# A second mixture whose conversions pass through a PSUM bank, and a table that paces them

## The chip, the cores and the metric

The kernel runs on one core of one Trainium2 chip. Its metric is the device time of one execution in microseconds. Three executions of the kernel before took 868.26, 870.14 and 873.36 us, with a median of 870.14.

## What is computed

Three blocks follow one another. Attention (4 batches, 8 heads, 576 positions, 64 wide) adds a strided and a local softmax; its output is a matrix x of 2304 tokens by 512. The first mixture has d_ff 768, the second 1536:

```python
def _moe_ref(x, w1, w2, w3, w_out) -> np.ndarray:
    h = np.maximum(np.maximum(x @ w1, x @ w2), x @ w3)
    return (h @ w_out).astype(np.float32)

def _moe2_ref(x, w_a, w_b, w_out) -> np.ndarray:
    a = x @ w_a
    b = x @ w_b
    return (a * b @ w_out).astype(np.float32)
```

Weights arrive as doubles (two 32-bit words each), and so have to be converted on the chip. Every float32 factor of a product is split in a rounded high part and a rest, so that three matmuls (high by high, rest by high, high by rest) stand for one.

## The kernel before

**Stages.** Attention runs to about 196 us with some first units of the first mixture under it. Then the order of instructions is written out by hand (`manual_schedule`, L1391). The first mixture works in quads (L1395): two chunks of 128 columns of d_ff by two blocks of 384 tokens, four units of three products `m1_p` (12 matmuls each), and the output of a quad by seven half-size products in two halves (`quad_out`, `product` L832), issued between the `m1_p` of the quad that follows. Before them `quad_forms` makes differences of the four hidden tiles y on VectorE (L762) and splits them on ScalarE and GpSimd (`part2`, L744, L745). Six quads are followed by four single units, the `rest` (L1396). In each `m1_unit` (L1446) a product is issued, then `tick(ticks[...])`, then outputs (`between`).

**Lanes.** What is not bound to a product stands in two lanes of generators (L636): conversions of weights, forms of weights (`quad_w`), forms of the second mixture's input (`sform`). `tick(n)` (L638) takes n steps from them, from one `yield` to the next, and so fixes where these instructions stand in the queues of VectorE, ScalarE and GpSimd. `need` (L657) takes steps until a missing piece is there. The numbers were FIRST (5 after each product of the first quad), MID and REST (L1436), and in the second mixture 1 or 2 after each product (`step`, `o`, L1519 to L1531).

**A conversion** (`convert_steps`, L509) of 128 by 512 doubles has four VectorE steps: two masks (L519 the exponent, L522 the mantissa into the tile `cm`), a multiply-add of the low word onto `cm` (L527) beside a ScalarE step on the exponent (L526), the sign (L529), and the product of mantissa and exponent (L536), into `cm` or into a tile `F` of forms. In the first mixture a cast on ScalarE (L630) and a rest on GpSimd (L632) are two further steps.

**The second mixture** (from about 445 us) runs 18 units of six blocks of d_ff by three pairs of token blocks. A unit (`m2_unit`, L1253) has seven products for each of the two weights j, in the order 1, 2, 6, 5, 7, 4, 3, six matmuls each (`prod`, L1052). Products 1, 6, 7 and 4 accumulate in a bank A (tag `ua`, two banks), 2 in a bank of its own, 5 and 3 in a bank E (both of tag `ub`, three banks in turn). `snap` (L1071) copies A to SBUF on ScalarE before the next product goes on in it. `m2_done` (L1078) adds bank and copy on VectorE: for j = 0 into `ca` (L1085), for j = 1 into `g` (L1095), and then multiplies `g` by `ca` (L1096). The hidden result is split (`m2_parts`, L1249, L1250) and multiplied by w_out one unit later (`m2_o`, tag `o`, three banks, added by VectorE at L1319). In all PSUM has eight banks: 2 `ua`, 3 `ub`, 3 `o`.

Every engine takes its instructions in the order of its queue. So a ScalarE copy that frees a bank for the next product can stand behind a step of a conversion that waits for VectorE.

## Time and profile before

| | before |
|---|---|
| median of three runs | 870.14 us |
| the profiled execution | 871.95 us |
| its span in the trace | 870.2 us |
| TensorE busy | 827.2 us, 95% |
| VectorE busy | 695.1 us, 80% |
| ScalarE busy | 357.7 us, 41% |
| GpSimd busy | 449.4 us, 52% |
| mean granted TensorE clock | 0.973 |

The span is the time from the first to the last instruction; 1.75 us lie around it. Busy times of matmuls overlap, since the trace models the end of each, so an idle TensorE in the trace was idle for a little longer in fact. An entry in square brackets is idle time of that engine just before the instruction, with the instruction that ended it.

### The profile page before, as it was taken

How to read it: one execution, taken by the hardware profiler on the slowest of the kernel's cores; microseconds unless marked ns; L12 is line 12 of the kernel's file. 1: busy time of each engine (PE TensorE's matmuls, PEld its weight loads, DVE VectorE, ACT ScalarE, POOL GpSimd, SP SyncE). 2: the span in 40 equal slices, each digit the busy share in tenths (PEclk: the TensorE clock that was granted, in tenths of full speed). 3: DMA queues.
4: the chain of work that ended last, by engine and by line, in shares of the span. 5: the costliest groups of instructions: out<-in, count | busy, mean ns of one | idle time of the engine just before them, and what ended most of it. 6: DMA issues, size and time to landing. Idle time of an engine off the chain costs nothing.

```text
span 870.2 us, 15404 instructions
## 1 busy us (share of the span) xinstructions
PE 827.2 (95%) x5785; PEld 772.2 (89%) x5785; DVE 695.1 (80%) x1220; ACT 357.7 (41%) x812; POOL 449.4 (52%) x417
## 2 busy tenths in 40 slices
PE   4898999999998999998998999999999999999998
PEld 3667788899898999997998899999999989999997
DVE  4799987666979588689589898999999865578885
ACT  3586655443333223324144554344434342343331
POOL 3776775544446237436357554545463563455541
PEclk9599899999999999999999999999999999999999
DMA  8977865310411113220134455445454449766612
GB/s 179 180 163 150 150 123 109 63 33 25 122 49 48 49 57 104 71 73 25 64 143 145 169 182 180 160 150 191 145 200 139 158 152 356 266 218 218 218 49 73
DMA packets 125557, 116.34 MB, mean 134 GB/s; under 512 B 81835, under 2 KB 108203, under 8 KB 125483
## 3 DMA queue, kind: packets, MB, share of 16 engines
q1 hardware_dynamic: 121162, 98.06, 38.7%
q10 hardware_dynamic: 4320, 17.30, 5.7%
q8 instruction: 45, 0.74, 0.4%
q14 instruction: 30, 0.24, 0.1%
HBM read 80.74 MB, written 34.60 MB: 133 GB/s over the span
## 4 chain that ended last, share of the span: by engine, by line
PE 69%; DVE 17%; DMA 4%; POOL 3%; issue 3%; ACT 2%; SPq 1%; DVEq 0%; POOLq 0%; ACTq 0%
PE ps_m L670 28%; PE ps_u L1061 25%; PE ps_m L1210 4%; PE ps_q L835 4%; DMA vr<-in_v_dram 3%; DVE cm L527 2%; DVE ce L529 2%; DVE cm L522 2%; DVE ce L519 1%; DVE cm L536 1%; PE ps_av L460 1%; PE ps_s L340 1%; PE ps_tl L423 1%; PE ps_sd L322 1%; PE ps_ud L438 1%
## 5 line engine op out<-in xcount | busy, mean ns | idle before, releaser
L670 PE MATMUL ps_m<-xh,w 128*128 128x384 f32 x864 | 175.0, 341 | 2.1 <-ACT t L696 1.6
L670 PEld LDWEIGHTS ps_m<-xh,w 128*128 128x128 f32 x864 | 152.4, 190 | 5.0 <-ACT t L696 2.7
L1061 PE MATMUL ps_u<-xh,w 128*128 128x384 f32 x720 | 137.5, 337 | 0.0
L1061 PEld LDWEIGHTS ps_u<-xh,w 128*128 128x128 f32 x720 | 125.8, 188 | 2.0 <-ACT sn L1073 0.6
L1061 PE MATMUL ps_u<-xl,w 128*128 128x384 f32 x648 | 123.9, 338 | 3.5 <-ACT sn L1073 3.5
L1061 PEld LDWEIGHTS ps_u<-xl,w 128*128 128x128 f32 x648 | 113.9, 189 | 5.6 <-ACT sn L1073 4.1
L1250 POOL TENSOR_TENSOR gl<-g,gh 128x384 fp32r<-128x384 f32 x52 | 58.6, 1127 | 82.0 <-ACT gh L1249 68.8
L670 PE MATMUL ps_m<-xl,w 128*128 128x384 f32 x432 | 94.6, 337 | 1.8 <-POOL xl L484 1.8
L670 PE MATMUL ps_m<-wo,gh 128*128 128x512 f32 (+1 forms) x316 | 93.1, 392 | 0.4 <-DVE acc L1319 0.4
L1073 ACT COPY sn<-ps_u 128x384 f32<-128x384 f32 x108 | 50.5, 478 | 97.6 <-PE ps_u L1061 97.4
L670 PEld LDWEIGHTS ps_m<-xl,w 128*128 128x128 f32 x432 | 76.3, 188 | 2.2 <-POOL xl L484 2.0
L670 PEld LDWEIGHTS ps_m<-wo,gh 128*128 128x128 f32 x316 | 58.6, 188 | 10.3 <-DVE acc L1319 0.8
L527 DVE SCALAR_TENSOR_TENSOR cm<-raw,cm 128x512 f32<-128x512 uint32 x60 | 64.1, 1069 | 1.5
L526 ACT ACTIVATE ce<-ce,ebias 128x512 int16<-128x512 uint16 x60 | 43.4, 723 | 46.8 <-DVE ce L519 46.6
L699 DVE TENSOR_TENSOR t<-ps_m,t 128x384 f32<-128x384 f32 x48 | 26.4, 551 | 44.5 <-PE ps_m L670 42.1
L992 POOL TENSOR_TENSOR w<-F,w 128x768 fp32r<-128x768 f32 (+1 forms) x36 | 56.8, 1592 | 4.9 <-ACT w L990 4.4
L1319 DVE TENSOR_TENSOR acc<-ps_m,acc 128x512 f32<-128x512 f32 (+1 forms) x67 | 44.8, 675 | 14.1 <-PE ps_m L670 14.0
L1003 POOL TENSOR_TENSOR F<-F 128x256 f32<-128x256 f32 x24 | 19.5, 815 | 65.3 <-DVE F L536 54.3
L670 PE MATMUL ps_m<-wo,gl 128*128 128x512 f32 (+1 forms) x158 | 48.9, 391 | 0.0
L1249 ACT CAST gh<-g 128x384 fp32r<-128x384 f32 x52 | 26.7, 514 | 52.9 <-DVE g L1096 49.2
L529 DVE SCALAR_TENSOR_TENSOR ce<-raw,ce 128x512 uint16<-128x512 uint16 x60 | 45.6, 760 | 2.5 <-ACT ce L526 2.5
L519 DVE TENSOR_SCALAR ce<-raw 128x512 uint16<-128x512 uint16 x60 | 45.2, 753 | 2.8 <-DMA raw<-in_moe_w_dram 2.8
(204 smaller groups left out, 1711.6 us busy)
## 6 DMA issues: line engine op xcount, KB each, us to landing
dw<-w SPq DMA_DIRECT2D x24, 768.0 KB
raw<-in_moe_w_dram SPq DMA_DIRECT2D x18, 512.0 KB
raw<-in_moe_w_out_dram SPq DMA_DIRECT2D x18, 512.0 KB
w<-dw SPq DMA_DIRECT2D x12, 768.0 KB
w<-dw ACTq DMA_DIRECT2D x12, 768.0 KB
dw<-wo SPq DMA_DIRECT2D x12, 512.0 KB
vw<-in_v_dram SPq DMA_DIRECT2D x62, 80.0 KB
vr<-in_v_dram SPq DMA_DIRECT2D x16, 288.0 KB
```

The lines of the kernel that those rows point to most:

```text
L519: nc.vector.tensor_scalar(out=e, in0=top, scalar1=0x7FF0, scalar2=None, op0=ALU.bitwise_and)
L526: nc.scalar.activation(out=s16, in_=e, func=AF.Relu, bias=ebias, scale=8.0)
L527: nc.vector.scalar_tensor_tensor(out=f, in0=lo, scalar=2.0**-32, in1=m, op0=ALU.mult, op1=ALU.add)
L529: nc.vector.scalar_tensor_tensor(out=e, in0=top, scalar=0x8000, in1=e, op0=ALU.bitwise_and, op1=ALU.bitwise_or)
L670: nc.tensor.matmul(ps, lhs[a], rhs[b], start=(i == 0), stop=(i == n - 1))
L835: nc.tensor.matmul(ps, sw[c0, n][a][:, m * P : (m + 1) * P], hq[n][b], start=start and k == 0, stop=k == 2, skip_group_check=not start,)
L992: nc.gpsimd.tensor_tensor(out=l, in0=w, in1=h.bitcast(F32), op=ALU.subtract)
L1061: nc.tensor.matmul(ps, w[:, a, slot, kk], y[:, b * HK + kk], start=start and i == 0, stop=i == 3 * HK - 1, skip_group_check=not start,)
L1073: nc.scalar.copy(t, ps)
L1210: nc.tensor.matmul(y, lhs[a], tw[c, n][b], start=start and k == 0 and t == ts.start, stop=k == 2, skip_group_check=True,)
L1250: nc.gpsimd.tensor_tensor(out=l, in0=g, in1=h.bitcast(F32), op=ALU.subtract)
L1319: nc.vector.tensor_tensor(out=a, in0=ps, in1=a, op=ALU.add)
```

## The change

There are three parts. First, once the first mixture has closed its banks, a pool of one PSUM bank (`cs`) is opened. The mantissa of a conversion is masked into that bank, the multiply-add goes on in it in place, and the last step writes from it to its target: the form tile `F`, or for w_out's pieces `cm` in SBUF. The exponent stays in SBUF. The bank comes from `ub`, which has two in place of three. Second, in `m2_done` for j = 1 the sum of bank and copy is written back into the bank, and the multiply reads it there; this holds for two of the three sums of a unit, not for (1, 1), whose bank goes on to accumulate. Third, the fixed numbers of `tick` are replaced by a table PACE of 330 entries, taken one after each product or output; when it has ended, the old numbers hold. 84 entries are the first mixture's, 21 each those of the first units of the second mixture, and those of units 3 to 6 are, in their effect, the old numbers.

```diff
@@ -46,6 +46,19 @@
 SUM_ACT = (0, 1, 2, 3, 4, 6, 7, 8, 9, 10, 13, 14, 15)
 NORM_POOL = (0, 1, 2, 3, 4, 5, 6, 7, 8, 9, 10, 11, 13, 14, 15)
 ADD_PSUM = range(16)
+
+
+PACE = (
+    14, 0, 4, 2, 5, 1, 3, 4, 2, 7, 1, 1, 2, 1, 0, 5, 5, 6, 1, 3, 5, 6, 4, 1, 0, 0, 1, 0, 4, 0, 4, 4, 1, 0, 3, 0,
+    0, 2, 0, 3, 8, 1, 1, 5, 0, 3, 4, 2, 0, 0, 0, 3, 7, 2, 5, 6, 3, 1, 0, 0, 0, 0, 3, 2, 4, 4, 2, 4, 7, 5, 1, 0, 1,
+    1, 0, 4, 1, 1, 8, 1, 4, 1, 5, 2, 1, 1, 0, 0, 3, 2, 4, 0, 0, 3, 0, 4, 0, 0, 2, 4, 0, 1, 0, 0, 0, 0, 5, 0, 4, 0,
+    0, 0, 2, 3, 6, 0, 1, 2, 0, 0, 3, 2, 1, 2, 0, 0, 0, 0, 1, 3, 0, 0, 7, 2, 0, 2, 2, 1, 3, 0, 1, 1, 1, 0, 1, 1, 0,
+    1, 1, 1, 1, 1, 1, 2, 2, 2, 2, 1, 1, 2, 2, 1, 1, 2, 2, 0, 0, 0, 1, 1, 1, 1, 1, 1, 2, 2, 2, 2, 1, 1, 2, 2, 1, 1,
+    2, 0, 1, 1, 0, 1, 1, 1, 1, 1, 1, 2, 2, 2, 2, 1, 1, 2, 2, 1, 1, 2, 2, 0, 0, 0, 1, 1, 1, 1, 1, 1, 2, 2, 2, 2, 1,
+    1, 2, 2, 1, 1, 2, 0, 1, 1, 0, 0, 4, 0, 4, 1, 0, 2, 1, 0, 4, 2, 0, 4, 1, 0, 0, 0, 1, 4, 2, 0, 0, 1, 3, 0, 1, 1,
+    4, 0, 0, 3, 3, 0, 0, 6, 0, 0, 2, 0, 0, 4, 0, 0, 1, 0, 2, 0, 2, 3, 0, 5, 1, 2, 1, 3, 1, 0, 0, 2, 1, 0, 1, 0, 2,
+    0, 0, 3, 3, 0, 0, 1, 0, 2, 1, 2, 3, 4, 0, 1, 1, 2, 2, 1, 0, 0, 1, 1, 1, 1, 0, 0, 0, 0, 0, 0, 0, 0, 0, 1,
+)
 
 
 @with_exitstack
@@ -514,7 +527,14 @@
         late_n[0] += "p" in late
         pl = late["p"] if late_n[0] % 2 else rawp
         e = pl.tile([P, NP_], U16, tag="ce", name="ce", bufs=CB)
-        m = pl.tile([P, NP_], U32, tag="cm", name="cm", bufs=CB)
+        fin = w
+        if w is None or "c" not in psp_:
+            m = pl.tile([P, NP_], F32, tag="cm", name="cm", bufs=CB)
+            if w is None:
+                fin = m
+        if "c" in psp_:
+            m = psp_["c"].tile([P, NP_], F32, tag="cs", name="ps_c", bufs=1)
+        m = m.bitcast(U32)
         s16, f = e.bitcast(I16), m.bitcast(F32)
         nc.vector.tensor_scalar(
             out=e, in0=top, scalar1=0x7FF0, scalar2=None, op0=ALU.bitwise_and
@@ -530,11 +550,11 @@
             out=e, in0=top, scalar=0x8000, in1=e, op0=ALU.bitwise_and, op1=ALU.bitwise_or
         )
         yield
-        out, i0, i1 = f if w is None else w, f, e.bitcast(BF16)
+        i0, i1 = f, e.bitcast(BF16)
         if w is not None and len(w.shape) == 3:
             i0, i1 = (x.rearrange("p (a b) -> p a b", a=w.shape[1]) for x in (i0, i1))
-        nc.vector.scalar_tensor_tensor(out=out, in0=i0, scalar=2.0**-20, in1=i1, op0=ALU.mult, op1=ALU.mult)
-        yield f
+        nc.vector.scalar_tensor_tensor(out=fin, in0=i0, scalar=2.0**-20, in1=i1, op0=ALU.mult, op1=ALU.mult)
+        yield fin
 
     def split(h, l, w):
 
@@ -653,6 +673,11 @@
             else:
                 return did
         return did
+
+    pace = iter(PACE)
+
+    def beat(n=0):
+        tick(next(pace, n))
 
     def need(has, key):
 
@@ -1091,9 +1116,10 @@
             g = gw[c % 2][:, x * TB : (x + 1) * TB]
         else:
             g = late["p"].tile([P, TB], F32, tag="g", name="g", bufs=2)
+        s = g if (i, b) == (1, 1) else ps
         if t is not None:
-            nc.vector.tensor_tensor(out=g, in0=ps, in1=t, op=ALU.add)
-        nc.vector.tensor_tensor(out=g, in0=ps if t is None else g, in1=ca.pop((i, b)), op=ALU.mult)
+            nc.vector.tensor_tensor(out=s, in0=ps, in1=t, op=ALU.add)
+        nc.vector.tensor_tensor(out=g, in0=s, in1=ca.pop((i, b)), op=ALU.mult)
         if strassen_o(c, p) and (i, b) == (0, 1):
             lanes[0].append(g_forms(c))
         else:
@@ -1264,7 +1290,7 @@
             T1[j] = snap(A[j])
             yield
         for j in range(2):
-            b = bank_u("ub", 3)
+            b = bank_u("ub", 2)
             prod(b, c, p, j, 2, True)
             m2_done(c, p, j, 0, 0, b, T1[j])
             yield
@@ -1273,7 +1299,7 @@
             T2[j] = snap(A[j])
             yield
         for j in range(2):
-            E[j] = bank_u("ub", 3)
+            E[j] = bank_u("ub", 2)
             prod(E[j], c, p, j, 5, True)
             yield
         for j in range(2):
@@ -1433,7 +1459,6 @@
         (5, 5): ("x", 5),
     }
     OUTS = (0, 4, 3, 3, 2, 2)
-    FIRST, MID, REST = (5,) * 12, (1, 1, 2, 2, 3, 3, 5, 5, 5, 5, 5, 5), (0, 0, 1, 3, 3, 3, 5, 5, 4, 2, 2, 2)
     outs, forms = None, None
 
     def between(n):
@@ -1443,14 +1468,14 @@
             next(outs)
         next(forms, None)
 
-    def m1_unit(u, steps, n, ticks):
+    def m1_unit(u, steps, n):
         for f in at_unit.get(u, ()):
             f()
         for j in range(3):
             next(steps)
             if j == 2 and n == 0 and outs is None and pending:
                 m1_o(*pending.pop())
-            tick(ticks[3 * n + j])
+            beat()
             between(3 * n + j)
         if u in after_unit:
             opened.add(after_unit[u])
@@ -1459,22 +1484,23 @@
         hq, y = {}, {}
         steps = quad(c0, c1, b0, b1, hq, y)
         for n, u in enumerate(((c0, b0), (c0, b1), (c1, b0), (c1, b1))):
-            m1_unit(u, steps, n, FIRST if c0 == 0 else MID)
+            m1_unit(u, steps, n)
         if outs is not None:
             assert next(outs, None) is None
         outs, forms = quad_out(c0, c1, b0, b1, hq), quad_forms(hq, y)
         next(forms)
     for n, u in enumerate(rest):
         steps = dense(u)
-        m1_unit(u, steps, n, REST)
+        m1_unit(u, steps, n)
         next(steps, None)
     for x in outs, forms:
         assert next(x, None) is None
     opened.add(("w", 2))
     m1_ps.close()
+    psp_["c"] = ctx.enter_context(tc.tile_pool(name="psc", bufs=1, space=PSUM, reuse_waits="tile"))
     psp_[2] = ctx.enter_context(tc.tile_pool(name="psm2", bufs=1, space=PSUM, reuse_waits="tile"))
 
-    psp_[2].tile([P, 512], F32, tag="ub", name="ps_u", bufs=3)
+    psp_[2].tile([P, 512], F32, tag="ub", name="ps_u", bufs=2)
 
     def spill(blk):
         y2[blk] = dram.tile([P, NK * TB], F32, tag=f"y2{blk}", name=f"y2{blk}")
@@ -1519,7 +1545,7 @@
         def step(m, k_=1):
             for _ in range(m):
                 part(lambda: next(unit, None))
-                tick(k_)
+                beat(k_)
 
         def one_o():
             while prev_o and next(prev_o[0], StopIteration) is StopIteration:
@@ -1528,7 +1554,7 @@
         def o(m):
             for _ in range(m):
                 part(one_o)
-                tick(2)
+                beat(2)
 
         step(3)
         if n == 0:
@@ -1567,7 +1593,7 @@
             for m in (0, 1, 1, 1, 2, 1, 1, 1):
                 step(m)
                 part(one_o)
-                tick()
+                beat(1)
             load_in(c + 2, 0)
             while prev_o:
                 part(one_o)
```

## Rows read from the trace of the kernel before

**Rows 1.** The page, part 1: busy us, share of the span, instructions.

```profile
PE 827.2 (95%) x5785; PEld 772.2 (89%) x5785; DVE 695.1 (80%) x1220; ACT 357.7 (41%) x812; POOL 449.4 (52%) x417
```

**Rows 2.** Windows by stage: width; busy us of each engine; granted clock; DMA share; GB/s.

```profile
196.00:285.00 89.00, 83.77 (x511) 80.52 (x510) 73.31 (x114) 34.19 (x71) 44.26 (x38) 1.00 0.20 60
...
390.00:500.00 110.00, 98.52 (x519) 94.79 (x518) 90.45 (x122) 42.58 (x77) 63.09 (x45) 0.95 0.30 108
500.00:690.00 190.00, 190.00 (x993) 176.83 (x993) 175.65 (x264) 81.97 (x154) 96.88 (x82) 1.00 0.48 172
690.00:710.00 20.00, 19.38 (x102) 17.62 (x101) 15.71 (x21) 9.14 (x17) 13.06 (x8) 1.00 0.21 68
```

**Rows 3.** Timeline of PE: start, us, line, out<-in, count, [idle before <-releaser].

```profile
236.57 0.62 PE L835 MATMUL ps_m<-hh,wo 128*128 128x384 f32 x2 [1.91 <-DVE y L699]
...
272.64 1.66 PE L670 MATMUL ps_m<-xh,w 128*128 128x384 f32 x8 [1.46 <-ACT t L696]
...
276.13 0.59 PE L835 MATMUL ps_q<-gh,w 128*128 128x384 f32 x2 [1.13 <-DVE acc L830]
...
410.09 0.58 PE L835 MATMUL ps_q<-gh,w 128*128 128x384 f32 x2 [3.40 <-DVE acc L830]
...
436.13 0.61 PE L670 MATMUL ps_m<-hh,wo 128*128 128x384 f32 x2 [2.76 <-DVE t L699]
...
460.95 3.50 PE L1061 MATMUL ps_u<-xl,w 128*128 128x384 f32 x12 [3.20 <-ACT sn L1073]
...
484.92 3.56 PE L1061 MATMUL ps_u<-ys,w 128*128 128x384 f32 x12 [1.99 <-ACT sn L1073]
```

**Rows 4.** Timeline of DVE: first step of a conversion, and the maximum after it.

```profile
232.26 0.42 DVE L519 TENSOR_SCALAR ce<-raw 128x512 uint16<-128x512 uint16 x1
...
235.96 0.55 DVE L699 TENSOR_TENSOR y<-ps_m,t 128x384 f32<-128x384 f32 x1
```

**Rows 5.** Timeline of ACT at 271 us.

```profile
271.18 0.62 ACT L630 CAST w<-cm 128x512 fp32r<-128x512 f32 x1 [3.66 <-DVE cm L536]
```

**Rows 6.** Timeline of DVE at 402 us.

```profile
402.15 0.55 DVE L699 TENSOR_TENSOR t<-ps_m,t 128x384 f32<-128x384 f32 x1
```

**Rows 7.** Timeline of DVE, 431 to 436 us.

```profile
431.07 2.08 DVE L522 TENSOR_SCALAR cm<-raw 128x512 uint32<-128x512 uint32 x1
...
435.52 0.55 DVE L699 TENSOR_TENSOR t<-ps_m,t 128x384 f32<-128x384 f32 x1
```

**Rows 8.** Timeline of ACT ahead of the snaps, 459 to 484 us.

```profile
459.81 0.72 ACT L526 ACTIVATE ce<-ce,ebias 128x512 int16<-128x512 uint16 x1 [5.13 <-DVE ce L519]
...
483.78 0.72 ACT L526 ACTIVATE ce<-ce,ebias 128x512 int16<-128x512 uint16 x1 [2.71 <-DVE ce L519]
```

**Rows 9.** Timeline of DVE, 456 to 479 us.

```profile
456.39 2.32 DVE L529 SCALAR_TENSOR_TENSOR ce<-raw,ce 128x512 uint16<-128x512 uint16 x1
...
473.38 1.62 DVE L1096 TENSOR_TENSOR g<-g,ca 128x384 f32<-128x384 f32 x1
...
476.46 2.22 DVE L536 SCALAR_TENSOR_TENSOR cm<-cm,ce 128x512 f32<-128x512 f32 x1
```

**Rows 10.** Groups by line and shape, DVE: count | busy us, mean ns | idle before.

```profile
L527 DVE SCALAR_TENSOR_TENSOR cm<-raw,cm 128x512 f32<-128x512 uint32 x60 | 64.1, 1069 | 1.5
...
L522 DVE TENSOR_SCALAR cm<-raw 128x512 uint32<-128x512 uint32 x60 | 44.9, 748 | 0.0
...
L1096 DVE TENSOR_TENSOR g<-g,ca 128x384 f32<-128x384 f32 x39 | 32.8, 841 | 1.3
...
L536 DVE SCALAR_TENSOR_TENSOR cm<-cm,ce 128x512 f32<-128x512 f32 x36 | 29.4, 817 | 0.6
...
L1096 DVE TENSOR_TENSOR g<-ps_u,ca 128x384 f32<-128x384 f32 x13 | 7.1, 547 | 1.5 <-PE ps_u L1061 0.7 <-POOL gl L1250 0.5 <-ACT ca L1083 0.3
```

**Rows 11.** Timeline at 703 us: a unit's products 2 (PE), the sum of the unit before (DVE).

```profile
703.04 2.24 PE L1061 MATMUL ps_u<-xh,w 128*128 128x384 f32 x12
...
703.21 0.54 DVE L1085 TENSOR_TENSOR ca<-ps_u,sn 128x384 f32<-128x384 f32 x1
```

## The prediction, made before the change was run

> **What bounds the kernel now.** The page first: TensorE is busy for 827.2 of 870.2 us, VectorE for 695.1 [rows 1]. So no edit of VectorE's work can be worth more than the time in which TensorE waits. The windows by stage say where that is [rows 2]. From 500 to 690 us TensorE is busy for 190.00 of 190 us: whatever VectorE saves there is worth nothing. Idle are 89.00 - 83.77 = 5.2 us at the start of the first mixture, 11.5 us from 390 to 500 and 0.6 us around 700. From 390 to 500 the granted clock is also 0.95 of full, against 1.00 around it; 0.05 of 110 us is 5.5 us at half its higher level, 1.2 in place of 2.4 GHz. Before 196 us nothing is edited. The timeline of TensorE then names the gaps [rows 3]: A 1.91 (at 236.6 us), B 1.46 and 1.13 (272 to 276), C 3.40 (410), D 2.76 (436), E 3.20 (461), F 1.99 (485). With G, the 0.62 near 700, that is 16.5 us of waiting, and with the slow clock 22 us: the ceiling of this change, unless it shortens TensorE's own work, which it doesn't touch. After C, E and F the clock is low; behind E and F twelve matmuls take 3.50 and 3.56 us [rows 3] where 2.24 is usual [rows 11], 1.3 us each in these alone. 5.5 us over three falls is at most 1.8 each; I take 1.6.
>
> Each gap is a queue: TensorE needs a bank, and the instruction that frees it stands on VectorE or ScalarE behind steps of a conversion or a form.
>
> **The table, gap by gap.** I count steps: a conversion of the first mixture has six, and one takes 235.96 - 232.26 = 3.7 us of VectorE [rows 4].
>
> A: the maximum that frees the bank ended at 236.5, right behind the sixth conversion of the first quad [rows 4]. The old numbers take all 49 steps that the first quad is offered. The table's first twelve entries (14, 0, 4, 2, 5, 1, 3, 4, 2, 7, 1, 1) sum to 44, one of which finds nothing to take, and leave six: just this conversion, which goes to 2, 1, 0, 5 behind the next quad's first products. The maximum comes 3.7 us earlier, more than the gap. Gain 1.9. What is late next is VectorE in the second quad, where 89.00 - 73.31 = 15.7 us are free in that stage [rows 2].
>
> B: the copy that frees the bank stands on ScalarE behind a weight cast, which waited 3.66 us for the last step of a conversion [rows 5]. The table (6, 4, 1 in place of 5, 5, 5 in the last unit of this quad) hands out only the second step of that conversion there, so the 1.46 should go. But VectorE has about the same work ahead of the differences, TensorE arrives 1.9 us earlier because of A, and then the sum that ends the 1.13 is awaited for longer. Of 2.6 I take 0.5; bounds 0 and 2.6.
>
> C: VectorE comes to a maximum of the last quad only at 402.15 [rows 6], because the input's forms and a conversion stand before it, and the differences and the sum that ends the gap come after it. The table gives two steps of a conversion, 1.07 for L527 [rows 10] and some 0.7 for L529, to the products before, but concentrates a form's three large steps and a conversion's last in one beat (2, 4, 7 in place of 5, 5, 5). All is still issued ahead of that maximum. I take 0.7 of 3.40; from -1.5 (bunching) to 3.4 plus its clock.
>
> D: one beat of five steps put a whole conversion (its second mask alone 2.08 us [rows 7]) ahead of the maximum at 435.52, with VectorE idle before it. The table gives 8, 1, 4: two steps of it come a product earlier, one stands there, the last follows. Two masks and the multiply-add, 2 x 0.75 + 1.07 = 2.6 us by their means [rows 10] and more by the 2.08 of this one, are out of the way: 2.8, the whole of D.
>
> **PSUM for mantissa and sums.** E and F are of another kind: TensorE waits for a snap on ScalarE, and the snap waits behind the exponent's step, which itself waited 5.13 and 2.71 us for VectorE's first mask [rows 8]. VectorE was late there because its instructions with both inputs in SBUF were drawn out beside a busy GpSimd: L529 took 2.32 us, L1096 1.62 and L536 2.22 [rows 9], the last two against means of 0.84 and 0.82 [rows 10]. The cost of an operand in PSUM can be read directly: the same multiply takes 841 ns with both factors in SBUF and 547 with one in PSUM [rows 10]. Of 36 multiplies (two in each of 18 units) each saves 0.294: 10.6 us. For a conversion's 512 columns I scale 547 by 512/384: 0.73, say 0.7. By the count of the table 30 of the 36 pieces of the second mixture are converted after the bank is opened; L522, L527 and L536 go from 748, 1069 and 817 ns [rows 10] to 0.7 each, 0.53 less, 16 us. Together 27 us off VectorE, nearly all beside a full TensorE. It counts only in the 11 us between 473 and 484: L1096 from 1.62 to 0.55 and L536 from 2.22 to 0.7 are 2.6 us, more than F's 1.99. For E there is the table too: in the first unit it spaces the next conversion over the pauses around products 5. I take F 2.0 + 1.6, and E 3.2 + 1.6 less 0.5 left over.
>
> No row shows VectorE writing to PSUM. Its price lies between the 547 of the read (0.73 scaled) and, if reading and writing one bank in place goes at half pace, twice that, 1.1 for a sum and 1.5 for a step of a conversion. I take the lower end, as L1096 is the nearest row; the upper end is a rival below.
>
> SBUF — State Buffer of the Trainium skill, section "Who interferes with whom", states that a VectorE instruction with at most one SBUF input and outside the two-port modes doesn't contend with GpSimd, and that otherwise the port pair is locked for a whole instruction. The 841 against 547 agrees. By that rule the exponent's mask L519 and its sign L529, which keep both sides in SBUF, go on waiting. VectorE: DVE Perf Modes, "Why PSUM operands drop a tier", speaks against the change: a mask into PSUM loses its double pace; by the 0.42 of the other mask in [rows 4] that would be 0.3 more for L522, 9 us less saved where VectorE isn't the limit.
>
> **The lost bank.** With two `ub` banks, product 2 of a unit takes the bank that product 3 of the unit before used, one product earlier than with three. The worst place I found is at 703: the product starts at 703.04, the sum that frees its bank ends at 703.75 [rows 11], a wait of 0.7. If three units had it, it would cost 2.1. With 27 us less on VectorE these sums come earlier. I set 1.0 for all new waits, those of bunched steps included, bounds 0 and 3. For G, where VectorE is late with w_out's sums, 0.4.
>
> **Sum.** 1.9 + 0.5 + 0.7 + 2.8 + 4.3 + 3.6 + 0.4 - 1.0 = 13.2 us. The profiled execution took 871.95 (span 870.2 and 1.75 around it), 0.2% above the median of 870.14. 871.95 - 13.2 = 858.7; on the median 856.9, so 857.
>
> **Rivals.**
> *All gaps go* (chance 0.12). B and C are freed too, and no bank is missed: 870.1 - 22 = 848. For it: VectorE has slack in every stage. Against: C's work is not reduced.
> *The wait moves* (0.17). GpSimd's instructions are as long as before, and what no longer waits in L527 or L536 waits in L519 and L529 next to them; L529 took 2.32 us [rows 9]. Then E and F stay, 7.5 of the 7.9 counted for them: 864.5. The Trainium skill's rule of the lock, named above, speaks for this.
> *The gaps only move* (0.07). Before 285 us and from 380 to 410 VectorE is the engine that is late, and handing out the same work elsewhere gives A back in B and lengthens C; with E or F staying, 868.
> *Slower: in place at half pace* (0.06). In the 190 us from 500 to 690 VectorE has 190.00 - 175.65 = 14.3 us free [rows 2]. At twice the price 24 conversions there cost (1.5 - 0.75) + (1.5 - 1.07) - 0.1 = 1.1 more each, 26 us, the 17 sums in place 0.55 each, 9 us, less 5 us of multiplies: 30. From 14.3 on VectorE is the limit, and the stage grows by some 16 us, with waits for `ub` in every unit. Less A and D: 870.1 + 16 - 4.7 = 881.
> The rest of the chance, 0.58, is the forecast's, with 851 to 863 as its own range.
>
> **How the numbers follow.** Under 0.5%, 4.4 us, this kernel can't be told from no change. Faster by more: the forecast, the first two rivals, less a share for values near the bound: 0.84. Within 0.5%: 0.10. Slower: 0.06. For 8 in 10 the range reaches over the forecast, half of the first rival and most of the second: 848 to 866.
>
> **What would show it.** A and D: no gap of TensorE over 0.5 us before 285 us but B's second, none between 425 and 440. E and F: no gap over 1 us from 450 to 490, a granted clock of at least 0.98 from 390 to 500. PSUM: L527 and L536 at 0.7 us with no spread, L1096 at 0.55 for all but the (1, 1) tiles, VectorE's sum below 675. Lost bank: no wait of `ps_u` for VectorE beyond 1 us in all. I would be wrong if C grew, if L519 and L529 took up what the others save, or if in-place sums took over 0.8.

## The result: 25 us shorter, nearly twice the forecast

| | before | after |
|---|---|---|
| median of four runs each | 871.75 us | 846.74 us |
| lowest and highest | 868.26 to 874.18 | 846.02 to 847.74 |
| span in the trace | 870.2 us | 845.9 us |
| mean granted TensorE clock | 0.973 | 0.980 |

The ratio is 0.9717, with a 95% interval of 0.9678 to 0.9756. The forecast was 857.0 with a range of 848 to 866: the direction held, the time lies 1.3 us below the range, and the sum, 13.2 us, found about half of the gain. It came out close to the rival in which all gaps go (848).

Lines of the kernel after: L519, L522, L526, L527, L529 and L536 of a conversion are L539, L542, L546, L547, L549 and L556; the maximum L699 is L724, its copy L696 L721, the differences L762 L787, the output sums L830 L855, the snap L1073 L1098, sum and multiply L1095 and L1096 L1121 and L1122, the matmuls L670, L835 and L1061 L695, L860 and L1086. In the experiments that carry a second table they lie 3 higher still.

The page of after, part 1 (busy us, share of the span, instructions) and the engines' shares of the chain of work that ended last:

```profile
PE 818.5 (97%) x5785; PEld 767.7 (91%) x5785; DVE 656.6 (78%) x1220; ACT 355.2 (42%) x812; POOL 444.0 (52%) x417
...
PE 85%; DMA 5%; POOL 4%; DVE 2%; SPq 2%; issue 1%; ACT 1%; POOLq 0%; DVEq 0%; ACTq 0%
```

VectorE has lost 38.5 us of its 695.1 [rows 1], and its share of the chain is 2%. Not all of this is PSUM's: by the pages of the two halves below, VectorE is busy for 672.3 us with PSUM alone and for 680.7 with the table alone, where the same instructions are only spaced otherwise. The same windows as before:

```profile
196.00:285.00 89.00, 88.63 (x546) 87.09 (x545) 72.03 (x119) 33.67 (x71) 44.76 (x38) 1.00 0.19 60
...
390.00:500.00 110.00, 108.73 (x597) 104.38 (x596) 87.09 (x142) 50.55 (x96) 69.50 (x53) 1.00 0.39 139
500.00:690.00 190.00, 190.00 (x998) 177.30 (x997) 155.66 (x258) 79.13 (x151) 97.58 (x80) 1.00 0.46 164
690.00:710.00 20.00, 20.00 (x102) 18.14 (x101) 9.32 (x15) 4.09 (x9) 4.38 (x5) 1.00 0.94 346
```

TensorE, the first busy time of each row, went from 83.77 to 88.63 of 89 us and from 98.52 to 108.73 of 110 us [rows 2], and the granted clock of the second stretch from 0.95 to 1.00. VectorE's 20 us less between 500 and 690 bought nothing: TensorE was full there already, and the starts compared below shift by 0.00 us there. What TensorE still waits for from 190 to 850 us, by the table of its waits (us in total, times, longest):

```profile
PE ps_m L695 <- DVE t L724: 0.7, 1, 0.7
PE ps_u L1086 <- ACT sn L1098: 0.4, 1, 0.4
PE ps_m L695 <- ACT xh L496: 0.3, 1, 0.3
```

1.4 us are left of some 17. No line has `ps_u` waiting for VectorE, so the lost `ub` bank shows no cost.

**What each gap gave.** Both kernels issue the same 5785 matmuls in the same order, so the start of the n-th in after can be set against the n-th in before; a step in this difference between two neighbours of a gap is what the gap gave. Starting from 196 us (attention is unchanged, and its end scatters by some us between executions). These are one trace of each kernel:

| place in before | forecast | measured | of it |
|---|---|---|---|
| A, 237 to 271 us | 1.9 | 3.6 | 2.1 at the gap, 1.5 in small waits behind it |
| B, 272 to 279 | 0.5 | 3.1 | 1.7 and 1.4 |
| C, 404 to 415 | 0.7 | 5.4 | 4.1 at the gap and just ahead of it, net of 0.2 lost at 377, and 1.3 slow clock behind it |
| D, 436 | 2.8 | 3.0 | |
| new waits, 437 to 450 | -1.0 | -1.3 | 0.9 for the maximum (the first line above, 0.7 of it idle), 0.3 and less |
| E, 461 to 466 | 4.3 | 4.4 | 2.9 and 1.5 slow clock |
| F, 485 to 490 | 3.6 | 3.8 | 2.2 and 1.6 slow clock |
| G and all behind it | 0.4 | 1.7 | 0.65, 0.55, 0.5 |

The rest of the 24.3 us between the spans, 0.6, is 1.1 in attention and behind the last matmul less a loss of 0.5 before 234 us, none of which the change explains.

**The price in PSUM.** VectorE's groups by line and shape in after (count | busy us, mean ns of one | idle before):

```profile
L549 DVE SCALAR_TENSOR_TENSOR ce<-raw,ce 128x512 uint16<-128x512 uint16 x60 | 49.8, 830 | 4.0 <-ACT ce L546 3.9
...
L539 DVE TENSOR_SCALAR ce<-raw 128x512 uint16<-128x512 uint16 x60 | 40.6, 677 | 2.2 <-DMA raw<-in_moe_w_dram 2.2
...
L547 DVE SCALAR_TENSOR_TENSOR cm<-raw,cm 128x512 f32<-128x512 uint32 x30 | 30.4, 1014 | 0.4
...
L1122 DVE TENSOR_TENSOR g<-ps_u,ca 128x384 f32<-128x384 f32 x39 | 21.7, 556 | 5.9 <-POOL gl L1276 1.1 <-issue 1.1 <-PE ps_m L1236 0.7
...
L547 DVE SCALAR_TENSOR_TENSOR ps_c<-raw,ps_c 128x512 f32<-128x512 uint32 x30 | 20.8, 692 | 0.7
L542 DVE TENSOR_SCALAR ps_c<-raw 128x512 uint32<-128x512 uint32 x30 | 20.5, 684 | 0.0
L1121 DVE TENSOR_TENSOR ps_u<-ps_u,sn 128x384 f32<-128x384 f32 x36 | 20.2, 562 | 10.2 <-PE ps_u L1086 10.2
...
L556 DVE SCALAR_TENSOR_TENSOR F<-ps_c,ce 128x512 f32<-128x512 f32 x20 | 13.8, 688 | 0.7
...
L1121 DVE TENSOR_TENSOR g<-ps_u,sn 128x384 f32<-128x384 f32 x13 | 7.2, 552 | 4.5 <-ACT sn L1098 4.5
```

Half of the conversions, those begun before the bank is opened (the first mixture's 24 and six of the second's 36), still have their mantissa in `cm` in SBUF: L547 costs 1014 ns there and 692 through the bank. A sum in place costs 562 ns, against 552 for the same sum written to SBUF and 547 for the multiply that only reads a bank [rows 10]. So the lower of the two bounds was right, and the rival at half pace is out.

### The profile page after: what moved, and what is told of

It reads as the page before. It is cut to its first block, busy times and chain, and to the rows that moved or that the text cites. A ratio compares the mean times of both kernels' runs of the same rounds, so it can differ in the third digit from the quotient of the medians.

```text
span 845.9 us, 15426 instructions
## 1 busy us (share of the span) xinstructions
PE 818.5 (97%) x5785; PEld 767.7 (91%) x5785; DVE 656.6 (78%) x1220; ACT 355.2 (42%) x812; POOL 444.0 (52%) x417
## 4 chain that ended last, share of the span: by engine, by line
PE 85%; DMA 5%; POOL 4%; DVE 2%; SPq 2%; issue 1%; ACT 1%; POOLq 0%; DVEq 0%; ACTq 0%
PE ps_m L695 39%; PE ps_u L1086 30%; PE ps_q L860 5%; PE ps_m L1236 4%; DMA vr<-in_v_dram 4%; PE ps_av L473 1%; PE ps_ud L451 1%; POOL vr L414 1%; PE ps_tl L436 1%; POOL el L403 1%; PE ps_sd L335 1%; PE ps_s L353 1%; PE ps_m L860 1%; DMA raw<-in_moe_w_dram 1%; PE ps_td L425 1%
## 5 line engine op out<-in xcount | busy, mean ns | idle before, releaser
L695 PE MATMUL ps_m<-xh,w 128*128 128x384 f32 x864 | 175.0, 341 | 0.3 <-ACT xh L496 0.3
L695 PEld LDWEIGHTS ps_m<-xh,w 128*128 128x128 f32 x864 | 152.8, 190 | 2.1 <-ACT xh L496 0.6
L1086 PE MATMUL ps_u<-xh,w 128*128 128x384 f32 x720 | 136.8, 336 | 0.1
L1086 PEld LDWEIGHTS ps_u<-xh,w 128*128 128x128 f32 x720 | 125.3, 188 | 1.9 <-DVE acc L751 0.4
L1086 PE MATMUL ps_u<-xl,w 128*128 128x384 f32 x648 | 122.4, 335 | 0.4 <-ACT sn L1098 0.4
L1086 PEld LDWEIGHTS ps_u<-xl,w 128*128 128x128 f32 x648 | 112.9, 188 | 2.2 <-ACT sn L1098 0.7
L1098 ACT COPY sn<-ps_u 128x384 f32<-128x384 f32 x108 | 51.1, 479 | 123.7 <-PE ps_u L1086 120.2
L1276 POOL TENSOR_TENSOR gl<-g,gh 128x384 fp32r<-128x384 f32 x52 | 55.4, 1066 | 82.3 <-ACT gh L1275 75.2
L695 PE MATMUL ps_m<-xl,w 128*128 128x384 f32 x432 | 95.2, 339 | 1.7 <-POOL xl L497 1.7
L695 PE MATMUL ps_m<-wo,gh 128*128 128x512 f32 (+1 forms) x316 | 92.4, 390 | 0.0
L695 PEld LDWEIGHTS ps_m<-xl,w 128*128 128x128 f32 x432 | 76.9, 189 | 2.1 <-POOL xl L497 2.0
L695 PEld LDWEIGHTS ps_m<-wo,gh 128*128 128x128 f32 x316 | 58.4, 188 | 9.6
L724 DVE TENSOR_TENSOR t<-ps_m,t 128x384 f32<-128x384 f32 x48 | 26.5, 551 | 45.6 <-PE ps_m L695 40.3
L546 ACT ACTIVATE ce<-ce,ebias 128x512 int16<-128x512 uint16 x60 | 43.4, 724 | 43.0 <-DVE ce L539 42.9
L1345 DVE TENSOR_TENSOR acc<-ps_m,acc 128x512 f32<-128x512 f32 (+1 forms) x67 | 44.9, 676 | 18.1 <-PE ps_m L695 17.9
L549 DVE SCALAR_TENSOR_TENSOR ce<-raw,ce 128x512 uint16<-128x512 uint16 x60 | 49.8, 830 | 4.0 <-ACT ce L546 3.9
L1110 DVE TENSOR_TENSOR ca<-ps_u,sn 128x384 f32<-128x384 f32 x54 | 30.0, 555 | 29.4 <-PE ps_u L1086 18.1
L695 PE MATMUL ps_m<-wo,gl 128*128 128x512 f32 (+1 forms) x158 | 48.9, 391 | 0.0
L1228 DVE TENSOR_TENSOR acc<-ps_m,acc 128x512 f32<-128x512 f32 (+1 forms) x62 | 33.3, 552 | 15.5 <-PE ps_m L1236 13.2
L539 DVE TENSOR_SCALAR ce<-raw 128x512 uint16<-128x512 uint16 x60 | 40.6, 677 | 2.2 <-DMA raw<-in_moe_w_dram 2.2
```

The lines of the kernel that those rows point to most:

```text
L539: nc.vector.tensor_scalar(out=e, in0=top, scalar1=0x7FF0, scalar2=None, op0=ALU.bitwise_and)
L546: nc.scalar.activation(out=s16, in_=e, func=AF.Relu, bias=ebias, scale=8.0)
L549: nc.vector.scalar_tensor_tensor(out=e, in0=top, scalar=0x8000, in1=e, op0=ALU.bitwise_and, op1=ALU.bitwise_or)
L695: nc.tensor.matmul(ps, lhs[a], rhs[b], start=(i == 0), stop=(i == n - 1))
L1086: nc.tensor.matmul(ps, w[:, a, slot, kk], y[:, b * HK + kk], start=start and i == 0, stop=i == 3 * HK - 1, skip_group_check=not start,)
L1098: nc.scalar.copy(t, ps)
```

## The experiments

Each edits the kernel after; OLD stands for the numbers of before written out as a table. The theory: the gaps A to D close by the table alone, E and F by what it and PSUM do together, and a gap costs more than the idle time printed beside it. The rivals: PSUM's relief of VectorE is the gain and the table only rides on it; or the table does all and PSUM is idle ornament. In these traces attention ends between 4.3 us earlier and 2.6 us later than in the trace of after, for no reason in the edits. So where medians lie close or their intervals overlap, what a part gives is read from the starts of matmuls behind attention. Only lines of each edit that matter are shown, `...` marks what is left out.

**The table alone, PSUM alone.** For the first, the sums and the mantissa go back to SBUF and the third `ub` bank returns; for the second, OLD replaces the table:

```diff
# e1_table_alone
-        s = g if (i, b) == (1, 1) else ps
+        s = g if t is not None else ps
...
-            b = bank_u("ub", 2)
+            b = bank_u("ub", 3)
...
-    psp_["c"] = ctx.enter_context(tc.tile_pool(name="psc", bufs=1, space=PSUM, reuse_waits="tile"))
...
# e2_psum_alone
...
+PACE = OLD
```

> Edit: of the change the table alone; mantissa and sums stay in SBUF, ub has three banks. Theory, that the table closes gaps A to D and PSUM closes E, F and G: the 16.5 us of waiting in the trace of before fall by A 1.9, B 2.6, C 3.4 and D 2.8, and C's fall of the clock (1.7) goes with it, so some 859 us; E and F stay with 3.2 and 2.0 and their low clock. Rival 1, that the table does nearly all: 847 to 849, no wait of TensorE over 1 us after 200 us. Rival 2, that the table only moves the waits without PSUM's relief: 866 or more.

> Edit: the changed kernel with the old numbers FIRST, MID, REST and 1 or 2 in place of the table; mantissa and sums in PSUM, ub two banks. Theory: everything before 445 us is as before, A to D stand with their 10.7 us, and E (3.2), F (2.0), G (0.6) and two falls of the clock go: some 862 us. Rival 1, that PSUM gives nothing that counts: 869 to 873, E and F as before. Rival 2, that the lost bank shows when VectorE runs on the old numbers: waits of ps_u for VectorE of 1 to 3 us in all.

The table alone took 855.59 us, a ratio of 0.9813 (0.9781 to 0.9844); PSUM alone 867.76, 0.9949 (0.9927 to 0.9970). Of the 25 us the table keeps 15.6 and PSUM 3.4; the last 6 need both. The first expectation, 859, was too cautious by 3 us, the second, 862, too hopeful by 6, as PSUM alone left E standing. TensorE's waits in the table's kernel (196 to 850 us) and in PSUM's (196 to 866 us):

```profile
PE ps_u L1086 <- ACT sn L1098: 5.5, 2, 3.6
...
```

```profile
PE ps_q L863 <- DVE acc L858: 4.5, 2, 3.4
PE ps_u L1089 <- ACT sn L1101: 3.2, 1, 3.2
PE ps_m L698 <- DVE t L727: 2.8, 1, 2.8
PE ps_m L863 <- DVE y L727: 1.9, 1, 1.9
PE ps_m L698 <- ACT t L724: 1.5, 1, 1.5
PE ps_u L1089 <- DVE ca L1113: 0.6, 1, 0.6
```

With the table alone the two lines left out are the first and last of after, 0.7 and 0.3, and A to D give the same hundredths as in after; so these are its work, and no VectorE saving is needed for them. With PSUM alone A to E stand as in before and of the large gaps only F is gone. That refutes the first rival; the 5.5 us left in the table's kernel (E at 1.9, F grown to 3.6) refute the second.

What F needs is PSUM: here are VectorE, ScalarE and TensorE with the table alone, up to the snap that TensorE waits for (start, us, instruction, [idle before]):

```profile
457.01 2.33 DVE L547 SCALAR_TENSOR_TENSOR cm<-raw,cm 128x512 f32<-128x512 uint32 x1
459.27 2.33 DVE L549 SCALAR_TENSOR_TENSOR ce<-raw,ce 128x512 uint16<-128x512 uint16 x1
461.63 1.38 DVE L556 SCALAR_TENSOR_TENSOR cm<-cm,ce 128x512 f32<-128x512 f32 x1
...
467.29 0.72 ACT L546 ACTIVATE ce<-ce,ebias 128x512 int16<-128x512 uint16 x1 [2.52 <-DVE ce L539]
...
468.43 4.21 PE L1086 MATMUL ps_u<-ys,w 128*128 128x384 f32 x12 [3.60 <-ACT sn L1098]
```

and the same stretch in after, with L547 of the next conversion too:

```profile
455.12 0.69 DVE L547 SCALAR_TENSOR_TENSOR ps_c<-raw,ps_c 128x512 f32<-128x512 uint32 x1
455.71 1.13 DVE L549 SCALAR_TENSOR_TENSOR ce<-raw,ce 128x512 uint16<-128x512 uint16 x1
456.87 0.69 DVE L556 SCALAR_TENSOR_TENSOR cm<-ps_c,ce 128x512 f32<-128x512 f32 x1
457.48 1.35 DVE L539 TENSOR_SCALAR ce<-raw 128x512 uint16<-128x512 uint16 x1
...
459.47 0.69 DVE L547 SCALAR_TENSOR_TENSOR ps_c<-raw,ps_c 128x512 f32<-128x512 uint32 x1
```

GpSimd is busy in both, with two differences of 768 columns: 4.41 us from 456.64 with the table alone, 4.31 from 456.24 in after. Beside them the steps that touch PSUM, L556 and the second L547, take 0.69, where beside GpSimd L547 took 2.33 in SBUF and L556 1.38 (the first L547 in after ran ahead of these differences, beside shorter GpSimd instructions); those that stay in SBUF, L549 and L539, take 1.13 and 1.35 and are still drawn out. The Trainium skill's SBUF — State Buffer, "Who interferes with whom", which the prediction weighed, has just this split, and the trace agrees; but what it left exposed was too short to hold up the snap.

Why E needs both: with PSUM alone the conversion ahead of E had been begun into `cm`, in SBUF:

```profile
456.32 1.51 DVE L550 SCALAR_TENSOR_TENSOR cm<-raw,cm 128x512 f32<-128x512 uint32 x1
457.76 2.32 DVE L552 SCALAR_TENSOR_TENSOR ce<-raw,ce 128x512 uint16<-128x512 uint16 x1
...
461.18 0.72 ACT L549 ACTIVATE ce<-ce,ebias 128x512 int16<-128x512 uint16 x1 [5.13 <-DVE ce L542]
```

The 2.32 and the 5.13 are those of before [rows 8, 9]. The bank can't help a conversion that was under way when it was opened; the table starts this one later, as a whole. So in after it goes through the bank (VectorE, then ScalarE's next exponent's step):

```profile
440.46 0.69 DVE L547 SCALAR_TENSOR_TENSOR ps_c<-raw,ps_c 128x512 f32<-128x512 uint32 x1
...
443.06 0.72 ACT L546 ACTIVATE ce<-ce,ebias 128x512 int16<-128x512 uint16 x1 [2.28 <-DVE ce L539]
```

With the table alone the same two read:

```profile
438.81 1.88 DVE L547 SCALAR_TENSOR_TENSOR cm<-raw,cm 128x512 f32<-128x512 uint32 x1
...
443.22 0.72 ACT L546 ACTIVATE ce<-ce,ebias 128x512 int16<-128x512 uint16 x1 [3.84 <-DVE ce L539]
```

**Which part of PSUM.** The mantissa's bank alone, the sums in place alone (with three `ub` banks), each with OLD and with the table, and the table with two `ub` banks and nothing in PSUM:

```diff
# e3_mantissa_alone: PACE = OLD;   e15_table_and_mantissa: the table
...
-        s = g if (i, b) == (1, 1) else ps
+        s = g if t is not None else ps
# e4_sums_alone: PACE = OLD;   e14_table_and_sums: the table
...
-            b = bank_u("ub", 2)
+            b = bank_u("ub", 3)
...
-    psp_["c"] = ctx.enter_context(tc.tile_pool(name="psc", bufs=1, space=PSUM, reuse_waits="tile"))
...
# e9_table_two_ub: e1 with bank_u("ub", 2)
```

> Edit: the old numbers, the mantissa of conversions in the PSUM bank, ub two banks, but sums in SBUF. Theory, that every VectorE step relieved counts at E and F by its share (in the stretch ahead of F one multiply gave 1.07 of 2.6 us, one conversion step 1.5): F shrinks from 2.0 to about 0.5, E less, some 865 to 866 us. Rival: only both together close F, 869 or more.

> Edit: the old numbers, the sums of products in place in PSUM, ub three banks, mantissa in SBUF. Theory: F shrinks from 2.0 to about 1, E stays, some 867 to 868 us. Rival: no effect outside the interval, since the conversions beside it take up the wait for GpSimd, 870 to 872.

> Edit: the changed kernel without the bank for the mantissa: table, sums in place in PSUM, ub three banks. The table alone leaves E with 2.1 us and F with 3.8 us and a long fall of the clock. Theory, that F was one multiply drawn out by GpSimd (with the old numbers the sums alone closed it): F is closed, E stays with 1.5 to 2 us, 848 to 850 us. Rival, that the mantissa is needed for F under the table's bursts: F 2 us or more, 852 to 855 us.

> Edit: the changed kernel with its sums in SBUF: table, mantissa in the PSUM bank, ub two banks. Theory, that the mantissa relieves the stretch ahead of E and a part of F (with the old numbers F stayed with 1.8 us): E under 1 us, F 1 to 2 us, 849 to 851 us. Rival, that either half of PSUM is enough: E and F closed, 847 us.

> Edit: the table, mantissa and sums in SBUF, but ub with two banks: against the table alone (855.6 us, three banks) this is the price of the lost bank while VectorE is not relieved. Theory: waits of ps_u for VectorE of 0.7 us in up to three units, 856 to 858 us. Rival, that the bank is never missed: 855.6 within the interval.

| | median, us | ratio to before, interval | E, us | F, us | F's copy done, us | TensorE there, us |
|---|---|---|---|---|---|---|
| OLD, nothing (before) | 871.19 | | 3.4 | 2.2 | 23.9 | 21.8 |
| OLD, mantissa | 868.18 | 0.9960 (0.9933 to 0.9986) | 3.4 | 1.8 | 22.1 | 20.3 |
| OLD, sums | 868.44 | 0.9962 (0.9940 to 0.9984) | 3.4 | closed | 23.0 | 22.9 |
| OLD, both | 867.76 | 0.9949 (0.9927 to 0.9970) | 3.4 | closed | 20.5 | 21.8 |
| table, nothing, 3 ub | 855.59 | 0.9813 (0.9781 to 0.9844) | 2.1 | 3.8 | 24.0 | 20.3 |
| table, nothing, 2 ub | 856.47 | 0.9816 (0.9786 to 0.9846) | 2.1 | 3.8 | 24.0 | 20.3 |
| table, sums | 854.58 | 0.9813 (0.9783 to 0.9843) | 2.1 | 2.8 | 23.1 | 20.3 |
| table, mantissa | 849.30 | 0.9761 (0.9715 to 0.9808) | 0.5 | 1.8 | 22.0 | 20.3 |
| table, both (after) | 846.74 | 0.9717 (0.9678 to 0.9756) | 0.5 | closed | 19.2 | 20.3 |

(E and F here from start to start of the two matmuls, less their usual distance. The last two columns count from the start of the matmul that ends E: when the copy that F waits for is done, and when TensorE could begin that matmul.) The gap F is about the difference of the last two columns, and only the first of them is PSUM's doing: with OLD and with the table the sums bring the copy forward by 0.9 and 1.0 us, near the prediction's 1.62 less 0.55 of a multiply [rows 9], the mantissa by 1.9 and 2.0, both together by 3.4 and 4.8. The second is the clock's. Behind E it was slow in before and in OLD with both, for longer in OLD with the sums, and not at all in OLD with the mantissa or in the kernels with the table; so TensorE came at 20.3, 21.8 or 22.9. That the sums closed F under OLD is half theirs and half luck: TensorE came 1.1 us later there than in before. Its trace, from attention's end on, is even 0.3 us longer than that of before, the time being lost to a slow clock behind C, D and E, though the median of ten gains 2.7. And the table alone doesn't delay the copy; F grew there because TensorE came 1.5 us earlier. Under the table the mantissa alone leaves as little of E as both do; F needs both. Two expectations failed here, 865 to 866 us for OLD and the mantissa and 848 to 850 for the table and the sums: they took the gap F of one trace for a measure of the copy alone.

The two rows with and without the third bank can't be told apart; in the trace with two banks one wait of 0.6 us for VectorE's `acc` is new. Under OLD the lost bank does cost: at 703 us, the place that the prediction named, the traces of both kernels with OLD and the mantissa have the `ca` wait shown above, 0.6 us, and that with OLD, the sums and three banks hasn't.

**Which part of the table.** Entries of before are put back for the second mixture, for the second quad, and for the sixth quad and its halves:

```diff
+PACE = PACE[:84]                            # e6_first_table_only
+PACE = PACE[:12] + OLD[12:24] + PACE[24:]   # e7_second_quad_old
+PACE = PACE[:60] + OLD[60:72] + PACE[72:]   # e5_quad6_old
+PACE = PACE[:66] + OLD[66:72] + PACE[72:]   # e10_forms_old
+PACE = PACE[:60] + OLD[60:66] + PACE[66:]   # e11_steps_old
```

> Edit: the changed kernel, of whose table the 84 entries of the first mixture are kept; the second mixture runs on the old 1 and 2. PSUM is on. Theory, that PSUM and the table of the first mixture close F, but E needs the spacing of the first unit's entries too: E leaves 1 to 3 us and perhaps a fall of the clock, 848 to 851 us. Rival 1, that the entries of the second mixture give nothing: 847. Rival 2, that without them PSUM can't hold E and F: 853 or more.

> Edit: the changed kernel, with the old 1, 1, 2, 2, 3, 3, 5, 5, 5, 5, 5, 5 in the second quad and the table elsewhere. Theory, that B is closed by the last three entries of this quad (6, 4, 1 for 5, 5, 5), which keep two steps of a conversion and the cast behind them off ScalarE's queue: waits of 1.5 and 1.1 us come back, some 849 to 850 us. Rival, that B is closed by VectorE's smaller backlog from the first quad: no wait, 847.

> Edit: the changed kernel, but the twelve entries of the sixth quad are the old 1, 1, 2, 2, 3, 3 and six 5s again. The two tables have handed out the same steps when this quad begins. Theory, that the spacing within this quad alone closes C: the wait of TensorE for VectorE's sum comes back with 3.4 us and a fall of the clock, 851 to 852 us, all other gaps stay closed. Rival, that C was closed because TensorE's and VectorE's delays from A and B no longer add up: C stays away, 847.

> Edit: the changed kernel, the sixth quad's first six entries from the table (0, 0, 3, 2, 4, 4), its last six the old 5s (for 2, 4, 7, 5, 1, 0). With the whole quad old, C came back with 3.6 us. Theory, that two steps of a conversion handed out ahead of the forms close C: it stays closed or under 1.5 us, 847 to 849 us. Rival, that the placing of the forms' own steps closes it (they then meet less of GpSimd's work, and the differences behind them take 3.4 us in place of 5.8): C is back with 3 us or more, 851 to 853 us.

> Edit: the reverse of the run before: the sixth quad's first six entries old (1, 1, 2, 2, 3, 3), its last six from the table. Theory, that the two steps ahead of the forms close C: the wait is back with 2 to 3.6 us, 850 to 853 us. Rival, that the placing of the forms' steps closes it: closed, 847 to 848 us.

*Second mixture old*: 850.47 us, 0.9733 (0.9691 to 0.9775), 3.7 above after. Three waits return, two near E and that for `ca` near 700:

```profile
PE ps_u L1089 <- ACT sn L1101: 1.8, 1, 1.8
PE ps_u L1089 <- ACT ca L1111: 0.9, 1, 0.9
...
PE ps_u L1089 <- DVE ca L1113: 0.6, 1, 0.6
```

So of the 330 entries the first mixture's 84 carry A to D and what they do for E; the other 246 are worth these 3 to 4 us: 2.6 from start to start near E and 1.1 near 700. The times alone would not show it: one of the four executions took 846.11, and the intervals overlap.

*Second quad old*: 850.78 us, 0.9750 (0.9704 to 0.9797), 4.0 above after, with executions from 846.82 to 854.68; from start to start the trace has 4.5 us more at B and 0.0 elsewhere behind attention. B is back though A stays closed (so the first quad's entries alone close A), as one gap, by the mechanism that [rows 5] show. ScalarE in this kernel, and TensorE's first wait:

```profile
269.32 0.62 ACT L653 CAST w<-cm 128x512 fp32r<-128x512 f32 x1 [2.77 <-DVE cm L559]
...
270.26 0.47 ACT L724 COPY t<-ps_m 128x384 f32<-128x384 f32 x1
```

```profile
PE ps_m L698 <- ACT t L724: 2.6, 1, 2.6
```

From 265 to 285 us the granted clock is 0.91 here. In after it is 1.00 in the whole stage.

*Sixth quad old*: 852.96 us, 0.9779 (0.9751 to 0.9808), 6.2 above after; its two halves 852.58, 0.9787 (0.9756 to 0.9818), and 851.96, 0.9781 (0.9757 to 0.9804). Waits for the output's sum at C in these three, in that order:

```profile
PE ps_q L863 <- DVE acc L858: 3.4, 1, 3.4
```

```profile
PE ps_q L863 <- DVE acc L858: 2.0, 1, 2.0
```

```profile
PE ps_q L863 <- DVE acc L858: 1.4, 1, 1.4
PE ps_m L863 <- DVE t L727: 1.2, 1, 1.2
```

The second line, a wait for the maximum itself, stands in the other two with 0.6 and 0.7. Of the three times' distances from after, 6.2, 5.8 and 5.2, none can be told from another. From start to start, from 390 to 425 us of before, the three need 7.6, 3.4 and 3.3 us more than after: with either half of the table in place, less than half is left. Part of the difference is the clock, which was slow behind the whole quad's gap (0.86 in the trace from 390 to 415) and at 1.00 behind those of the halves. So what counts is the spacing of the whole quad. The expectation that the two steps ahead of the forms close C by themselves failed. VectorE up to the maximum and the differences in after:

```profile
389.64 0.68 DVE L556 SCALAR_TENSOR_TENSOR F<-cm,ce 128x512 f32<-128x512 f32 x1
...
393.87 0.54 DVE L724 TENSOR_TENSOR t<-ps_m,t 128x384 f32<-128x384 f32 x1
...
396.10 1.26 DVE L787 TENSOR_TENSOR y<-y,t 128x384 f32<-128x384 f32 x1
397.29 1.01 DVE L787 TENSOR_TENSOR y<-y 128x384 f32<-128x384 f32 x2
```

and in the last kernel, whose first half of the quad has the old numbers:

```profile
390.68 0.41 DVE L542 TENSOR_SCALAR ce<-raw 128x512 uint16<-128x512 uint16 x1
...
397.80 0.54 DVE L727 TENSOR_TENSOR t<-ps_m,t 128x384 f32<-128x384 f32 x1
...
399.98 2.67 DVE L790 TENSOR_TENSOR y<-y 128x384 f32<-128x384 f32 x2
```

There a whole conversion, from its first mask on, stands behind the input's forms and ahead of the maximum; in after only its last step. In before the maximum of 402.15 [rows 6] came 0.56 us behind the start of the outputs' first matmul, at 401.59; in after it comes 1.07 ahead of that matmul's start, at 394.94. That is 1.6 us earlier. Behind it the last three differences took 2.08 and 2.62 us in before and take 1.26 and 1.01 here, 2.4 us less. GpSimd was busy beside all of them in before (4.68 us from 401.38, then 2.58 from 406.01); in after its 2.56 us difference ends at 395.65 and it is idle for 1.04 us among them. So this second part came with where GpSimd's work fell. The five kernels agree. In this table, in us, stand the start of the maximum, counted from the start of the outputs' first matmul; the four differences behind it in sum; how much both together exceed those of after; and how much longer than in after the stretch from 390 to 425 us of before is:

| sixth quad | maximum | differences | both, over after | stretch, over after |
|---|---|---|---|---|
| after | -1.1 | 3.4 | | |
| before | 0.6 | 5.8 | 4.1 | 5.6, clock slow behind it |
| whole quad old | 1.2 | 5.8 | 4.7 | 7.6, clock slow behind it |
| last six old | 1.3 | 4.4 | 3.4 | 3.4 |
| first six old | 1.8 | 3.8 | 3.3 | 3.3 |

So the lateness of the maximum and the length of the differences are what TensorE waits for at C. That GpSimd's overlap and nothing else makes the differences long was not tried by itself.

## Why the prediction was right, and where it was wrong

**Right.** The gaps were the ceiling, TensorE's own work didn't change, and what VectorE saves from 500 to 690 us is worth nothing. D, E, F and the new waits came within 0.3 us of their terms. E and F go by the mechanism given, a snap behind an exponent's step behind VectorE. The forecast named the table and PSUM for E, which needs both, and for F the sums and L536, which PSUM alone bears out; that F without PSUM would grow once E's slow clock is gone was not seen. For D that it was this beat was not tried by itself. VectorE's total, forecast below 675, is 656.6; but PSUM alone took 22.8 us off, under the 27 counted, and the rest came by the table's spacing, which had no term. L547, L556 and L1122 have the 0.69 and 0.56 us that were named. The Trainium skill's VectorE: DVE Perf Modes, "Why PSUM operands drop a tier", was right on the mask: L542 takes 0.684 us into PSUM and 0.42 undisturbed in SBUF (at 467.17 us of the table's kernel). Even so it is cheaper through the bank than the mean of 748 ns that it had [rows 10].

**C, 0.7 against 5.4.** This is the term that failed most. The two steps of a conversion were seen to move, and they brought the maximum 1.6 us forward, near the 1.07 and 0.7 that the prediction gave them. What failed is the value set on it: "All is still issued ahead of that maximum" was taken as a reason to cut the gain to 0.7, for fear of bunching. The differences behind the maximum were left at the length they had; they shrank by 2.4 us when GpSimd's long one no longer ran beside them (that this is the reason was not tried by itself). And the slow clock behind C, 1.3, was in the ceiling and in no term, though E and F had theirs. 1.6 + 2.4 + 1.3 = 5.3. The halves of the quad's entries, neither enough without the other, say the same: it was decided over the whole quad and not at the beat next to the gap.

**B, 0.5 against 3.1.** The step "TensorE arrives 1.9 us earlier because of A, and then the sum that ends the 1.13 is awaited for longer" was a guess at what is late next, and with the table nothing was. With the second quad at its old numbers B came back though A stayed closed; with the table it did not. B was bound to its own beats.

**A, 1.9 against 3.6, and G, 0.4 against 1.7.** The term was the idle time that one row prints. From start to start A was worth 2.1, and 1.5 us of small waits behind it, none over 0.4 us, went with it. The text under the table of before says that an idle TensorE is idle for a little longer than printed; no term had that. This is also why the ceiling of 22 us was too low: the seven gaps gave 25.0 with their clock.

**New waits, -1.0 against -1.3.** The size was right by luck, the cause wrong: no `ub` wait, but one for a maximum where the first mixture ends, 0.9 from start to start, which every kernel with the table has. The `ub` wait at 703 exists where the old numbers stand, and the table takes it away.

**The rivals.** All gaps go: this is what happened, though its 848 came near in part by luck, from a ceiling of 22 us where the gaps gave 25.0 and new waits took 1.3. The argument against it, that C's work is not reduced, was true and beside the point, as it was moved. The wait moves to L519 and L529: they are 677 and 830 ns long now, before 753 and 760, so L529 took up a little and nothing moved in sum. The gaps only move: no. That the work counted need not shrink for a gap to close is the lesson of A, B and C together.

## What to carry to other kernels

Where one engine is full and its gaps are waits for copies in another engine's queue, count what stands ahead of each copy over the whole group of products and not in the beat next to it; moving steps within the group can close a gap without any work being saved. Price a gap from start to start of the two instructions around it, with the clock and the small waits behind it, not by the idle time printed beside it. And test two parts of a change apart and together: here 15.6 and 3.4 us alone were 25.0 in one.

## What the hardware showed beyond that

VectorE reading and writing one bank in place took the time of the same instruction undisturbed in SBUF: 0.69 us for L547 in both (in SBUF at 463.72 us of the table's kernel). The gain of the bank is not a cheaper instruction but one that was not drawn out beside a busy GpSimd: 0.69 against 2.33 us for the same step beside the same two differences of GpSimd. For the mask L542 it is dearer, 0.68 against 0.42.

The granted clock did not follow a gap's length alone. It fell behind gaps in before (C, E, F; 0.93 from 390 to 415 and 0.92 from 457 to 500 us) but not behind D's 2.76 us there, nor behind the 2.0 and 1.4 us left of C with half of the sixth quad old. With OLD and the mantissa, and with OLD and the sums, D's gap is the same 2.76 us, and behind it the clock fell (0.89 and 0.77 from 430 to 445 us, 1.00 in before); so the same wait is sometimes paid for twice and sometimes not, and the slow clock's parts in the tables above are those of these traces. With the table alone, twelve matmuls behind the 3.60 us of F took 4.21 us in place of 2.25, and the granted clock was 0.85 from 457 to 480 us. Between 1.2 and 2.4 GHz a wait is paid for a second time; which wait it will be, these runs don't tell.
